# The last block's output projection by seven half-size products, and softmax sums moved to the head of their visit

## Chip, core and metric

The kernel runs on one core of a Trainium2 chip. The metric is the device time of one execution in microseconds (us). A core has five engines that run their own instruction streams in order and meet through semaphores: PE (matrix products), DVE (elementwise vector work), ACT (activations and copies), POOL (here broadcasts over partitions, and loads), and SP (here it only issues transfers). The profile shows PE's weight loads apart, as PEld.

## The reference

Linear attention in the style of Linformer, then a gated feed-forward layer. Batch 8, 8 heads, sequence 1024, head size 64; K and V are projected along the sequence to 64 rows.

```python
k_proj = np.einsum('ks,bhsd->bhkd', E, k)
v_proj = np.einsum('ks,bhsd->bhkd', F, v)
scores = scale * np.matmul(q, k_proj.transpose(0, 1, 3, 2))
attn = softmax(scores)            # over the 64 projected rows
x = np.matmul(attn, v_proj)       # heads side by side: 8192 tokens x 512
gate = 1.0 / (1.0 + np.exp(-(x @ w_gate)))
val = x @ w_val                   # 512 -> 1536, both
out = gate * val @ w_out          # 1536 -> 512, float32
```

## The kernel before

**Tiles and blocks.** The 8192 tokens are 16 blocks of 512, two blocks to a batch; `o1 = 2 * b` is the first block of batch `b`. For a block, the gate `x @ w_gate` is twelve groups of four 128x512 matmuls (`g_step`), and the value and output products are done by Strassen's scheme in Winograd's form: a 2x2 block product from seven half-size products instead of eight. For the value product these are `v_product` pieces (`p1`, `p26`, `p57`, `p4`, `p3`, lines 1461 to 1499). For the output product they are `product` calls of 12 matmuls with 256 columns each, in `first_products` and `last_products` (lines 1295 to 1328).

**Operands of the output product.** The hidden activations `hT` of a block are split into quarters: `A11`, `A21` hold the first 768 hidden features for tokens 0 to 255 and 256 to 511, `A12`, `A22` the other 768. `s_sums` (line 1214) makes four sums on DVE: S1 = A21 + A22, S2 = S1 - A11, a third that replaces A21 by A11 - A21 in place, and a fourth that replaces A12 by A12 - S2 in place. The sums can be made for part of the rows: `A = (0, 4)` for four of six row tiles, `Z = (4, 6)` for the last two. The matching sums T1 to T4 of `w_out` are made once. Partial results are taken out of PSUM as snapshots (`keep_snap`, ACT) and added to the output tile `ost` on DVE (`add_snap`, line 1277). Before the change the last block alone, number 15, uses plain products instead: `oproj` (line 1163) with 12 matmuls of 512 columns for each of four groups of 128 tokens, the fourth split into 384 and 128 columns.

**Order of the work.** Nothing is scheduled by a planner: the program is written out in order, each helper appends its instruction to its engine's stream, and `Plan` (line 28) works out the semaphore waits from keys that are read and written. The main loop (line 1610) runs `b` from 1 to 7. One iteration has six units of nine slots: `g_step` and the `v_product` pieces alternate, and `on(u, j, fn)` hangs further work behind slot `j` of unit `u`. In iteration `b`, this work is the output products of blocks `2b - 1` and `2b`, and the attention of batch `b + 1`, for `b` up to 6.

**The visit.** `outputs3` (line 1055) is hung on `on(3, 0, ...)`. On PE it issues the attention outputs `xo_one` for two head pairs, the softmax sums `den8`, and, in iterations 1 to 5, the K and V projection `kv` of the batch after. ACT copies the attention outputs to `xu` (`x_half`). DVE takes the reciprocals of the sums (`rec`, line 838). Then eight small transfers on SP bring the reciprocals to rows (`gather`), POOL broadcasts them over partitions (`spread`, line 912), and DVE multiplies `xu` by them into `xT` (`mul`, line 945), from slot (4, 4) on. `xT` is what the next batch's feed-forward reads. Ahead of `outputs3` in the same slot stand the `Z` sums of block `2b` (line 1657), three DVE instructions.

**Banks.** `FF` and `AA` are lists of free PSUM banks, four each. `take` pops the first; a bank is put back when its reader has been issued.

Of the kernel before, what the change touches and what calls it, by code (L numbers as in the profile page):

```python
# [7 lines left out]
ALU = mybir.AluOpType  # L8
# [9 lines left out]
DM = 512  # L18
# [100 lines left out]
def bass_linformer_attn__then__ffn_glu_sigmoid_kernel(  # L119
# [11 lines left out]
    B = q.shape[0]  # L131
# [6 lines left out]
    with contextlib.ExitStack() as es:  # L138
# [71 lines left out]
        ost = sbuf("ost", [P, 4, DM], FP32)  # L210
# [13 lines left out]
        add = plan.add  # L224
# [29 lines left out]
        FF, AA = Free(), Free()  # L254
# [15 lines left out]
        def dve(fn, r, w, b=None):  # L270
            x = [] if b is None else [("bank", b)]
            return add("DVE", fn, r=r, w=w, x=x)
# [525 lines left out]
        def attention(b):  # L798
# [127 lines left out]
            def xo_one(r, bks):  # L926
                for g in range(2):
                    n = 2 * r + g
                    for c in range(2):
                        kk = slice(64 * (g ^ c), 64 * (g ^ c) + 64)  # L930
                        mm(
                            bks[g],
                            bank[bks[g]][64 * c : 64 * c + 64, :],
                            vpD[kk, 2 * r + c, :],
                            eT[kk, n, :],
                            VPD(r // 2) + [("eT", n)],
                            tp=(64 * (g ^ c), 64 * c),
                        )
# [115 lines left out]

            def outputs3():
                f, a0 = FF.two(), AA.two()
                xo_one(2, f)
                xo_one(3, a0)
                bd = AA.take()
                den8(bd)  # L1060
                if b + 1 < B:
                    held["kv"] = AA.take()
                    kv(b + 1, held["kv"])
                for g in range(2):
                    x_half(2, g, f)
                    FF.append(f[g])
                later("A0", x_half, 3, a0, AA)
                rec(0)
                rec(1)
                AA.append(bd)  # L1070
                gather()
                spread(0)
                spread(1)
# [161 lines left out]
                return [(x, m) for m in up]  # L1235
            return [("hT", blk % 2, m + H6 * (x[2] == "2"), int(x[1]) - 1) for m in up]

        def product(blk, bk, A, B, start=False, stop=False):
            h = hT[blk % 2]
            for j in range(2):  # L1240
                for m in range(H6):
                    if A[0] == "S":
                        lhsT = hS[:, int(A[1]) - 1, m, j * P : (j + 1) * P]
                    else:
                        c = 256 * (A[1] == "2") + j * P
                        lhsT = h[:, m + H6 * (A[2] == "2"), c : c + P]
                    if B[0] == "T":
                        rhs, k = wT[:, int(B[1]) - 1, m, :], ("wT", int(B[1]) - 1)
                    else:
                        c = 256 * (B[2] == "2")  # L1250
                        rhs, k = wO[:, m + H6 * (B[1] == "2"), c : c + 256], "wO"
                    mm(
                        bk,
                        bank[bk][:, 256 * j : 256 * j + 256],
                        lhsT,
                        rhs,
                        part(blk, A, [m]) + [k],
                        start=start and m == 0 and j == 0,
                        stop=stop and m == H6 - 1 and j == 1,
                        read=True,  # L1260
                    )

# [50 lines left out]
        def last_products(blk):  # L1313
            a, c = chain
            product(blk, a, "A22", "T4", stop=True)
            o, keys = quarter(1, 0)
            act(o, bank[a][:, :].rearrange("p (j c) -> p j c", j=2), [], keys, b=a, scale=0.5)
            product(blk, c, "A12", "B22", stop=True)
            add_snap(1, c, 0, 1)
            AA.extend(chain)  # L1320
            for tt in (2, 3, 0, 1):
                t = 2 * (2 * (blk % 2) + tt % 2) + tt // 2
                add(
                    "SP",
                    lambda e, tt=tt, t=t: e.dma_start(out_v[blk // 2, t], ost[:, tt, :]),
                    r=[("ost", tt, n) for n in range(2)],
                    dma=f"out{tt}",
                )

# [278 lines left out]
        for b in range(1, B):  # L1610
            todo, at = [], {}
            for u in range(6):
                K = 6 * b + u
                p1, p26, p57, p4, p3 = v_pieces(K)
                todo += [
                    last_piece,
                    p1,
                    lambda K=K: g_step(K, 1),
                    p26,
                    lambda K=K: g_step(K, 2),  # L1620
                    p57,
                    lambda K=K: g_step(K, 3),
                    p4,
                    (lambda K=K: g_step(K + 1, 0)) if K + 1 < 6 * B else (lambda: None),
                ]
                last_piece = p3

            def on(u, j, fn):
                put(9 * u + j, fn)

            def h_sums(blk, ms, *ns):
                return lambda: [s_sums(blk, n, ms) for n in ns]

            def x_sums(blk, *ns):
                return lambda: [xs_sums(blk, n) for n in ns]

            A, Z = (0, 4), (4, 6)
            o0, o1 = 2 * b - 1, 2 * b
            if b == 1:
                first = {1: lambda: (vt_sums(1), vt_sums(4), x_sums(2, 1, 2, 3, 4)())}  # L1640
                on(0, 0, lambda: first_products(o0, first))
                on(0, 2, lambda: last_products(o0))
                on(0, 4, x_sums(3, 1, 2, 3, 4))
                on(2, 0, h_sums(o1, A, 1))
                on(2, 4, h_sums(o1, A, 2, 3))
            else:
                on(0, 4, h_sums(o0, A, 1, 2))
                on(1, 0, h_sums(o0, A, 3))
                on(1, 0, h_sums(o0, Z, 1))
                on(1, 4, h_sums(o0, Z, 2, 3))  # L1650
                first = {
                    0: x_sums(o1 + 1, 1, 2, 3, 4),
                    1: h_sums(o1, A, 1, 2, 3),
                }
                on(2, 0, lambda: first_products(o0, first))
                on(2, 2, lambda: last_products(o0))
            on(3, 0, h_sums(o1, Z, 1, 2, 3))
            if b + 1 < B:
                n = attention(b + 1)
                late, keep_kv, mul = n["late"], n["keep_kv"], n["mul"]  # L1660
                ks = 1 if b == 1 else 0
                for u, name in ((ks, "scores"), (ks + 1, "mixed")):
                    on(u, 0, n[name])
                    on(u, 1, lambda: late("A0", 0))
                    on(u, 3, lambda: late("A0", 1))
                    on(u, 6, lambda: (late("A1", 0), late("A1", 1)))
                on(3, 0, n["outputs"])
                on(3, 1, lambda: late("A0", 0))
                on(3, 3, lambda: late("A0", 1))
                on(3, 6, lambda: keep_kv(0))  # L1670
                on(4, 1, lambda: keep_kv(1))
                on(4, 3, lambda: keep_kv(2))

                on(4, 4, lambda: (mul(0, 0), mul(0, 1)))
                last = {
                    -1: lambda: mul(1, 0),
                    0: lambda: (mul(1, 1), mul(2, 0), mul(2, 1)),
                    1: lambda: (mul(3, 0), mul(3, 1)),
                }
                on(5, 0, lambda: first_products(o1, last))  # L1680
                on(5, 4, x_sums(o1 + 2, 1, 2))
                on(5, 7, x_sums(o1 + 2, 3, 4))
            else:
                on(5, 0, lambda: first_products(o1))
            on(5, 2, lambda: last_products(o1))
            if b + 2 < B:
                kpd_ = [("kpD", R) for R in range(2)] if b == 1 else []
                load_at = (1, 4) if b == 1 else (0, 2)
                on(*load_at, lambda: (load_k(b + 2, kpd_), load_v(b + 2), load_q(b + 2)))
                on(3, 4, transpose_q)  # L1690
            for i, slot in enumerate(todo):
                slot()
                for fn in at.pop(i, ()):
                    fn()
            assert not at
        last_piece()
        last = 2 * B - 1
        for tt in range(4):
            oproj(
                last,  # L1700
                tt,
                FF.take(),
                ((0, DM),) if tt < 3 else ((0, 384), (384, DM)),
            )

        plan.emit(nc, es, final=[f"out{i}" for i in range(4)] + ["outlast"])

# [26 lines left out]
```

## Time and profile before

| quantity | value |
| --- | --- |
| median of 7 runs | 535.78 us (534.55 to 536.32) |
| the profiled execution: its time | 535.89 us |
| the profiled execution: its span, first to last instruction | 534.1 us |
| PE busy | 521.4 us, 98% |
| DVE, ACT, POOL busy | 404.5, 300.6, 133.3 us |
| granted TensorE clock | 1.000 |

The rest of the profiled time beside the span lies before the first and after the last instruction. In a timeline line the columns are start (us from the span's start), duration (us), engine, source line, operation, output and inputs by name, shapes, how many instructions are merged, and in brackets the engine's idle time before them with what ended it. `SPq` is an issue of a transfer by SP, not the transfer. Almost all matmuls have line 264 and are told apart by their tiles: `pF<-xT,wG` is the gate, `pF<-xS,wV` and the like the value product, `pA<-wT,hS` and the like the output product, `pA<-eT,dsel` the softmax sums, `pF<-eT,vpD` the attention outputs, `pA<-KVs,EFT` the projection of K and V. A matmul's duration includes its way through the array, so starts, not ends, show PE's pace.

### The profile page before, as it was taken

The numbers are of one execution on the slowest core, as the hardware profiler recorded it, in microseconds if no ns is written. First come the engines' busy times: TensorE is split into PE (matmuls) and PEld (weight loads), VectorE is DVE, ScalarE is ACT, GpSimd is POOL, SyncE is SP. The second block draws the span as 40 slices with busy tenths as digits, with TensorE's granted clock in tenths as the row PEclk, the third lists the DMA queues.
The fourth block names the chain that finished last, engine by engine and source line by source line (L and its number), as shares of the span: only waits on it lengthen the run. The fifth ranks groups of instructions, "written<-read, shape, count | busy, mean of one in ns | idle before, by whom it ended". The sixth has DMA issues, their size and how long they took to land.

```text
span 534.1 us, 10316 instructions
## 1 busy us (share of the span) xinstructions
PE 521.4 (98%) x4113; PEld 344.4 (64%) x4113; DVE 404.5 (76%) x655; ACT 300.6 (56%) x540; POOL 133.3 (25%) x148
## 2 busy tenths in 40 slices
PE   5999999999999999999999999999999999999998
PEld 4544446656857667585766768576675856767674
DVE  3646386888987788877988789878888789887733
ACT  2554732687385564946567473755748464544540
POOL 9310200104800076001930048100650009200000
PEclk9999999999999999999999999999999999999999
DMA  9999999893295254921679223962520010202022
GB/s 167 199 192 202 162 201 217 148 180 64 37 225 84 79 92 71 227 57 45 91 154 162 80 45 56 202 108 80 91 80 1 14 69 3 79 1 80 1 79 80
DMA packets 76768, 56.18 MB, mean 105 GB/s; under 512 B 34800, under 2 KB 68528, under 8 KB 76720
## 3 DMA queue, kind: packets, MB, share of 16 engines
q0 software_dynamic: 33984, 29.89, 36.0%
q1 hardware_dynamic: 42736, 25.63, 19.7%
q8 instruction: 32, 0.52, 0.4%
q14 instruction: 16, 0.13, 0.1%
HBM read 60.29 MB, written 16.78 MB: 144 GB/s over the span
## 4 chain that ended last, share of the span: by engine, by line
PE 89%; DVE 5%; DMA 3%; POOL 1%; issue 1%; ACT 0%; DVEq 0%; POOLq 0%
PE pF L264 59%; PE pA L264 30%; DMA KVs<-in_v_dram 2%; DVE xT L949 2%; DVE vsnap L1435 2%; POOL KVs L917 1%; DVE rden L841 1%; DVE hT L1150 0%; POOL KVs L282 0%; DMA eT<-rden 0%; POOL Qb L282 0%; DVE hT L1416 0%; ACT vsnap L268 0%; DVE hS L1228 0%; DVE rden L639 0%
## 5 line engine op out<-in xcount | busy, mean ns | idle before, releaser
L264 PE MATMUL pF<-xT,wG 128*128 128x512 bf16 x768 | 197.9, 379 | 0.3
L917 POOL PARTITION_BROADCAST KVs<-eT x96 | 96.5, 1032 | 246.2 <-PE pF L264 193.4
L268 ACT ACTIVATE sig<-pF 128x512 f32<-128x512 f32 x192 | 115.6, 602 | 52.9 <-PE pF L264 50.9
L1435 DVE TENSOR_TENSOR vsnap<-pF,vsnap 128x512 f32<-128x512 f32 x126 | 86.7, 688 | 38.0 <-PE pF L264 27.5
L264 PEld LDWEIGHTS pF<-xT,wG 128*128 128x128 bf16 x768 | 73.7, 98 | 57.1 <-issue 1.7
L268 ACT ACTIVATE vsnap<-pF 128x512 f32<-128x512 f32 x126 | 75.3, 598 | 49.7 <-PE pF L264 46.9
L1416 DVE SCALAR_TENSOR_TENSOR hT<-sig,vsnap 128x512 bf16<-128x512 f32 x126 | 88.3, 701 | 6.2 <-ACT vsnap L268 0.5
L264 PE MATMUL pF<-xT,wV 128*128 128x256 bf16 (+1 forms) x432 | 76.1, 297 | 0.3 <-DVE hT L1150 0.3
L264 PE MATMUL pA<-wO,hT 128*128 128x256 bf16 x504 | 59.6, 273 | 0.0
L264 PEld LDWEIGHTS pF<-xT,wV 128*128 128x128 bf16 x432 | 40.6, 98 | 28.2 <-issue 4.9
L264 PEld LDWEIGHTS pA<-wO,hT 128*128 128x128 bf16 x504 | 49.3, 98 | 5.9
L264 PE MATMUL pF<-xS,wV 128*128 128x256 bf16 x336 | 50.5, 273 | 2.6 <-DVE vsnap L1435 2.0
L949 DVE TENSOR_TENSOR xT<-xu,KVs 128x512 bf16<-128x512 f32 x48 | 47.5, 1028 | 6.6 <-POOL KVs L917 6.6
L264 PE MATMUL pF<-xS,vT 128*128 128x256 bf16 x336 | 50.4, 273 | 0.0
L264 PEld LDWEIGHTS pF<-xS,wV 128*128 128x128 bf16 x336 | 31.9, 98 | 26.9 <-DVE vsnap L1435 9.0
L268 ACT ACTIVATE EF<-pA 128x512 f32<-128x512 f32 x28 | 16.7, 598 | 45.3 <-PE pA L264 45.3
L264 PE MATMUL pA<-wT,hT 128*128 128x256 bf16 x336 | 41.3, 273 | 0.0
L264 PE MATMUL pA<-wT,hS 128*128 128x256 bf16 x336 | 39.0, 273 | 0.0
L264 PEld LDWEIGHTS pA<-wT,hT 128*128 128x128 bf16 x336 | 32.9, 98 | 6.8
L264 PEld LDWEIGHTS pF<-xS,vT 128*128 128x128 bf16 x336 | 32.9, 98 | 3.8
L264 PEld LDWEIGHTS pA<-wT,hS 128*128 128x128 bf16 x336 | 32.5, 98 | 4.2
L1150 DVE SCALAR_TENSOR_TENSOR hT<-sig,pF 128x512 bf16<-128x512 f32 x24 | 16.4, 688 | 23.3 <-PE pF L264 11.2
(109 smaller groups left out, 501.8 us busy)
## 6 DMA issues: line engine op xcount, KB each, us to landing
out_dram<-ost SPq DMA_DIRECT2D x60, 256.0 KB, 2.5
Qb<-in_q_dram POOLq DMA_DIRECT2D x7, 1024.0 KB, 20.5
KVs<-in_k_dram POOLq DMA_DIRECT2D x7, 1024.0 KB, 12.7
KVs<-in_v_dram POOLq DMA_DIRECT2D x7, 1024.0 KB, 16.4
wO<-in_moe_w_out_dram POOLq DMA_DIRECT2D x1, 1536.0 KB, 13.0
wG<-in_moe_w_gate_dram POOLq DMA_DIRECT2D x5, 256.0 KB, 18.0
wV<-in_moe_w_val_dram POOLq DMA_DIRECT2D x5, 256.0 KB, 18.6
KVs<-in_k_dram POOLq DMA_DIRECT2D x2, 512.0 KB, 8.9
```

The lines of the kernel that those rows point to most:

```text
L264: return add("PE", lambda e: e.matmul(o, lhsT, rhs, **kw), r=r, x=[("bank", b)])
L268: return add("ACT", lambda e: e.activation(o, i, func, scale=scale), r=r, w=w, x=x)
L841: lambda e: e.reciprocal(rden[:, cc], bank[bk][:, cc]),
L917: lambda e, n=n, i=2 * rnd + c, j=j, parts=parts: e.partition_broadcast(rb[0:parts, n, :], rrow[32 * j : 32 * j + 1, i, :], channels=parts),
L949: lambda e: e.tensor_tensor(xT[s][:, r, :, 256 * g : 256 * g + 256], xu[:, n, :].rearrange("p (f c) -> p f c", f=2), y.rearrange("p (f c) ...
L1150: lambda e: e.scalar_tensor_tensor(hT[blk % 2][:, m, :], sg, 1.0, bank[pv][:, :], ALU.add, ALU.mult,),
L1416: lambda e: e.scalar_tensor_tensor(o, sg[:, :, cc], 1.0, x.rearrange("p (j c) -> p j c", j=2), ALU.add, ALU.mult,),
L1435: lambda e: e.tensor_tensor(o, bank[bk][:, :], o, ALU.add),
```

## The change

Three things are changed. In `outputs3`, `den8` is issued ahead of both `xo_one`. The `Z` sums of block `2b` are appended after `outputs3`, so that on DVE they follow the reciprocals; in iteration 6 they are hung four slots later; in iteration 7, which has no attention, they stay. And block 15 is done by seven products too: its operand sums are made inside iteration 7, and `final_products` takes the place of `oproj`. Its order differs from the other blocks': it uses five banks, one product of A12 and B22 is issued in two halves (`js`), each into a bank of its own, and the output leaves in eight stores of 128 rows by 256 columns instead of five.

```diff
--- before.py
+++ after.py
@@ -1054,10 +1054,10 @@
 
             def outputs3():
                 f, a0 = FF.two(), AA.two()
+                bd = AA.take()
+                den8(bd)
                 xo_one(2, f)
                 xo_one(3, a0)
-                bd = AA.take()
-                den8(bd)
                 if b + 1 < B:
                     held["kv"] = AA.take()
                     kv(b + 1, held["kv"])
@@ -1235,9 +1235,9 @@
                 return [(x, m) for m in up]
             return [("hT", blk % 2, m + H6 * (x[2] == "2"), int(x[1]) - 1) for m in up]
 
-        def product(blk, bk, A, B, start=False, stop=False):
+        def product(blk, bk, A, B, start=False, stop=False, js=(0, 1)):
             h = hT[blk % 2]
-            for j in range(2):
+            for j in js:
                 for m in range(H6):
                     if A[0] == "S":
                         lhsT = hS[:, int(A[1]) - 1, m, j * P : (j + 1) * P]
@@ -1255,8 +1255,8 @@
                         lhsT,
                         rhs,
                         part(blk, A, [m]) + [k],
-                        start=start and m == 0 and j == 0,
-                        stop=stop and m == H6 - 1 and j == 1,
+                        start=start and m == 0 and j == js[0],
+                        stop=stop and m == H6 - 1 and j == js[-1],
                         read=True,
                     )
 
@@ -1326,6 +1326,54 @@
                     r=[("ost", tt, n) for n in range(2)],
                     dma=f"out{tt}",
                 )
+
+        def final_products(blk):
+
+            a, b, c, e0 = [AA.take() for _ in range(4)]
+            e1 = FF.take()
+
+            def store(tt, col, sem):
+                t = 2 * (2 * (blk % 2) + tt % 2) + tt // 2
+                cc = slice(256 * col, 256 * col + 256)
+                add(
+                    "SP",
+                    lambda e: e.dma_start(out_v[blk // 2, t][:, cc], ost[:, tt, cc]),
+                    r=[("ost", tt, col)],
+                    dma=sem,
+                )
+
+            def plus(o, keys, n, bk, jj):
+                dve(
+                    lambda e: e.scalar_tensor_tensor(
+                        o, bank[bk][:, jj], 0.5, snap[n][:, jj], ALU.mult, ALU.add
+                    ),
+                    [("snap", n)],
+                    keys,
+                    b=bk,
+                )
+
+            product(blk, a, "A11", "B11", True)
+            keep_snap(0, a)
+            product(blk, c, "S1", "T1", True, True)
+            product(blk, a, "S2", "T2")
+            keep_snap(1, a)
+            plus(snap[1], [("snap", 1)], 1, c, slice(0, 512))
+            product(blk, b, "A12", "B21", True, True)
+            s_sums(blk, 4, (0, 6))
+            add_snap(0, b, 0, 0)
+            product(blk, a, "A21", "T3")
+            keep_snap(2, a)
+            add_snap(2, c, 1, 1)
+            product(blk, e0, "A12", "B22", True, True, (0,))
+            plus(ost[:, 0, 256:512], [("ost", 0, 1)], 1, e0, slice(0, 256))
+            product(blk, a, "A22", "T4", stop=True)
+            o, keys = quarter(1, 0)
+            act(o, bank[a][:, :].rearrange("p (j c) -> p j c", j=2), [], keys, b=a, scale=0.5)
+            product(blk, e1, "A12", "B22", True, True, (1,))
+            plus(ost[:, 1, 256:512], [("ost", 1, 1)], 1, e1, slice(256, 512))
+            for tt, col in ((0, 0), (1, 0), (2, 1), (3, 1), (0, 1), (2, 0), (3, 0)):
+                store(tt, col, f"out{tt}")
+            store(1, 1, "outlast")
 
 
 
@@ -1654,7 +1702,6 @@
                 }
                 on(2, 0, lambda: first_products(o0, first))
                 on(2, 2, lambda: last_products(o0))
-            on(3, 0, h_sums(o1, Z, 1, 2, 3))
             if b + 1 < B:
                 n = attention(b + 1)
                 late, keep_kv, mul = n["late"], n["keep_kv"], n["mul"]
@@ -1665,6 +1712,7 @@
                     on(u, 3, lambda: late("A0", 1))
                     on(u, 6, lambda: (late("A1", 0), late("A1", 1)))
                 on(3, 0, n["outputs"])
+                on(3, 0 if b + 2 < B else 4, h_sums(o1, Z, 1, 2, 3))
                 on(3, 1, lambda: late("A0", 0))
                 on(3, 3, lambda: late("A0", 1))
                 on(3, 6, lambda: keep_kv(0))
@@ -1681,7 +1729,10 @@
                 on(5, 4, x_sums(o1 + 2, 1, 2))
                 on(5, 7, x_sums(o1 + 2, 3, 4))
             else:
-                on(5, 0, lambda: first_products(o1))
+                on(3, 0, h_sums(o1, Z, 1, 2, 3))
+                last = {1: h_sums(o1 + 1, A, 1, 2, 3)}
+                on(5, 0, lambda: first_products(o1, last))
+                on(5, 7, h_sums(o1 + 1, Z, 1, 2, 3))
             on(5, 2, lambda: last_products(o1))
             if b + 2 < B:
                 kpd_ = [("kpD", R) for R in range(2)] if b == 1 else []
@@ -1694,14 +1745,7 @@
                     fn()
             assert not at
         last_piece()
-        last = 2 * B - 1
-        for tt in range(4):
-            oproj(
-                last,
-                tt,
-                FF.take(),
-                ((0, DM),) if tt < 3 else ((0, 384), (384, DM)),
-            )
+        final_products(2 * B - 1)
 
         plan.emit(nc, es, final=[f"out{i}" for i in range(4)] + ["outlast"])
 
```

## The prediction

> **What bounds the kernel now.** I read the page first (busy shares, chain), then the timeline around one attention visit of the main loop (iteration 4) and around the last one (iteration 6), then the end of the program. From the page:
>
> ```profile
> span 534.1 us, 10316 instructions
> ...
> PE 521.4 (98%) x4113; PEld 344.4 (64%) x4113; DVE 404.5 (76%) x655; ACT 300.6 (56%) x540; POOL 133.3 (25%) x148
> ...
> PE 89%; DVE 5%; DMA 3%; POOL 1%; issue 1%; ACT 0%; DVEq 0%; POOLq 0%
> ```
>
> PE is the bound, so an edit pays only where PE issues fewer columns or stands still. Standstill is read from start times: twelve 256-column matmuls occupy 1.31 us (one product starts at 421.13, its follower at 422.44), four 512-column ones 0.87 (422.88 to 423.75); anything beyond that before the next start is a stall. The usual visit (timeline, iteration 4):
>
> ```profile
> 308.77 1.76 DVE L841 RECIPROCAL rden<-pA 128x128 f32<-128x128 f32 x2
> ...
> 310.56 5.56 SPq L904 DMA_DIRECT2D eT<-rden  x8
> ...
> 311.17 0.69 DVE L1435 TENSOR_TENSOR vsnap<-pF,vsnap 128x512 f32<-128x512 f32 x1 [0.64 <-PE pF L264]
> ...
> 319.17 2.21 DVE L949 TENSOR_TENSOR xT<-xu,KVs 128x512 bf16<-128x512 f32 x2
> ```
>
> Here the `vsnap` add after the reciprocals waits 0.64 for PE, so their place costs nothing, and the first `xT` multiply has no wait for POOL. PE loses only 0.23 us after the multiplies (512-column group at 320.94, +0.87 = 321.81, next start 322.04). The last visit (iteration 6) has no K/V projection behind it, 1.9 us of PE work elsewhere:
>
> ```profile
> 434.24 1.76 DVE L841 RECIPROCAL rden<-pA 128x128 f32<-128x128 f32 x2
> ...
> 434.96 1.03 PE L264 MATMUL pF<-xT,wG 128*128 128x512 bf16 x4
> ...
> 435.92 0.63 DVE L1435 TENSOR_TENSOR vsnap<-pF,vsnap 128x512 f32<-128x512 f32 x1
> 436.03 5.58 SPq L904 DMA_DIRECT2D eT<-rden  x8
> ...
> 436.61 0.61 PE L264 MATMUL pF<-xS,wV 128*128 128x256 bf16 x4 [0.62 <-DVE vsnap L1435]
> ...
> 439.99 0.95 POOL L917 PARTITION_BROADCAST KVs<-eT  x1 [45.29 <-issue]
> ...
> 444.36 2.10 DVE L949 TENSOR_TENSOR xT<-xu,KVs 128x512 bf16<-128x512 f32 x2 [0.70 <-POOL KVs L917]
> ...
> 446.38 0.68 DVE L1435 TENSOR_TENSOR vsnap<-pF,vsnap 128x512 f32<-128x512 f32 x1
> ...
> 447.11 0.61 PE L264 MATMUL pF<-xS,wV 128*128 128x256 bf16 x4 [0.79 <-DVE vsnap L1435]
> ```
>
> PE stalls twice: 434.96 + 0.87 = 435.83 against 436.61, 0.78 us; and (group at 445.30) 446.17 against 447.11, 0.94 us. Both hang on the reciprocals: the first because the add queues behind them, the second through gather, broadcast, multiply (which did wait 0.70 for POOL) and the add behind the multiplies. The end (timeline, then SP's last issue):
>
> ```profile
> 520.90 10.55 PE L264 MATMUL pF<-wO,hT 128*128 128x512 bf16 x60
> ...
> 524.49 7.80 SPq L1191 DMA_DIRECT2D out_dram<-ost  x5
> ...
> 530.90 0.89 DVE L1181 TENSOR_SCALAR ost<-pF 128x384 f32<-128x384 f32 x2 [1.26 <-PE pF L264]
> ```
> ```profile
> 531.86 0.43 SPq L1191 DMA_DIRECT2D out_dram<-ost  x1
> ```
>
> So what counts at the end is when SP can start its last store, 531.86; the span ends 2.2 us later.
>
> **What the Trainium skill says.** "TensorE: Matmul & The Clock Gate", Back-to-back issue gap, gives N/2.4 + 2.5 ns: 109 and 216 ns for 256 and 512 columns; the trace has 1.31/12 = 109 and 0.87/4 = 217. "Perfetto Trace Analysis", DMA Instruction — HWDGE (DVE, Sync): SP is held from semaphores met until descriptors are made, then is free. The trace agrees: stores start 300.49 and 300.87, taking 0.33 and 0.43, so about 0.38 then 0.48 us a store back to back. "DMA: Bandwidth & Descriptors", Anatomy of one DMA: most of the fixed time is the write receipt; the trace's 64 KB store lands in 1.7 us, the 256 KB ones in 2.5, so small stores keep their tail. "SBUF — State Buffer", Who interferes with whom: a DVE instruction with two SBUF inputs collides with a GpSimd one that reads SBUF; the `xT` multiplies take 1.14 us (median) in the broadcasts, 0.68 at least without.
>
> **The change, part by part.**
> *den8 ahead of xo, six visits.* Same matmuls, same number of changes of tile shape (about 0.1 us each: the 16 den8 matmuls start at 306.76, kv at 307.31). The xo products, and the ACT copies of `xu`, come 0.55 us later; ACT's next work in iteration 4 is at 309.86, and in iteration 6 its queue catches up by 435.2. Cost 0; unhidden, 0.55 in a visit.
>
> *Reciprocals ahead of the operand sums (five visits), sums to a later slot (sixth).* The three sums cost DVE 1.13 us (433.11 to 434.24); the reciprocals start that much earlier: den8's result is there by about 432.3, DVE's previous instruction lets go at 433.11. In iterations 1 to 5 the add's 0.64 us wait for PE covers the exchange, and the multiplies are placed by DVE, not POOL. Gain 0; I bound it at -0.1 to +0.1 a visit (the broadcasts now begin 1.1 us earlier, over other two-input instructions).
> In iteration 6 the add goes from 435.92 to 434.79, ends 435.47, before PE's 435.83: the 0.78 goes. All eight gather issues, and so the broadcasts, come 1.13 earlier. PE is 0.78 earlier, so the second stall shrinks by 1.13 - 0.78 = 0.35, to about 0.59. The sums land behind the next `hT` multiply, from 436.0 to 437.1, where DVE then waits for ACT anyway (0.97 us before, 437.34 to 438.32); the following add can start at 437.54 either way. If that cover failed, PE would meet it when bank c is needed again, 0.65 us further on. Gain 1.13; bounds 0.6 (half the sums come through) and 1.72 (both stalls gone).
>
> *Sums of block 15.* Four-row sums, 3 x 0.69 = 2.05 us, go where DVE waits 2.60 us (513.87 to 516.47): 0. The two-row sums, 1.13 us, precede DVE's last two `vsnap`/`hT` steps; `A12` is then whole at about 524.1 and is read at 525.3: 0.
>
> *Last block.* Removed: 36 x 512, 12 x 384, 12 x 128 columns; added: 84 x 256. PE issue: 520.90 to 531.29 (10.39) becomes 84 x 0.109 = 9.17. Step by step from 520.90, 1.31 each: A11 to 522.21, S1 523.52, S2 524.83, A12·B21 526.14, A21 527.45. The sum that rewrites `A12` waits for PE (0.30 from product end to DVE start, as at 508.42 and 508.72), 526.44 + 0.95 = 527.39: just in time for the half product, 528.10. A22·T4 needs the third snapshot: 527.45 + 0.20 + 0.60 = 528.25, a stall of 0.2. It ends 529.61, the second half product 530.27. DVE's last add, 256 wide (between 0.29 for 128 and 0.56 for 384, I take 0.43), 530.47 to 530.90.
> SP now has eight stores instead of five: ready at 528.03 (two), 528.97 (two), 529.3 (one), 530.45 (two, from ACT: 529.61 + 0.2 + 0.6), 530.90. With 0.38 and 0.48 spacing: 530.48, 530.86, and the last at 531.34 instead of 531.86: 0.5 earlier; its 128 KB queue behind less data than the 192 KB before, I add 0.1. Gain 0.6 of PE's 1.22; bounds 0.75 (SP never waits) and -0.2 (0.6 us an issue, as the gather's: 529.0 + 5 x 0.6 = 532.0).
>
> Sum: 1.13 + 0.6 = 1.73 on the profiled 535.89, 534.16; the median of the runs is 0.11 lower, so **534.05 us**.
>
> **Rivals.** (a) *The stores take the last block's gain.* At 0.57 us an issue the last starts at 529.0 + 2.85 = 531.85, as before. For: the eight gather issues take 5.58, some spaced 0.59. Against: those carry waits for one another, stores show 0.38 to 0.5. Time 535.78 - 1.13 = 534.65.
> (b) *The moved sums or late `xu` copies come through in iteration 6*, 0.5 us of the 1.13 lost. Against: the 0.97 of DVE idle. Time 534.55.
> (c) *Slower: the store queue outright.* From 0.80 us an issue (5 x 0.80 + 529.0 = 533.0) the end loses more than the 1.13 gained; at 1.1 us, 534.5 for the last store, 2.6 later: 535.78 - 1.13 + 2.6 = 537.3. For it: only SP's transposes take over 1.2 us; plain stores never.
> (d) *The usual visits gain too*, the 0.23 stall gone in each of five: 534.05 - 1.15 = 532.9. Against: nothing there waits for POOL.
> (e) *The last block's dependent tail costs more* (each product waits for its snapshot), gain 0: near 534.65 too, with (a).
>
> **How the numbers follow.** Forecast 0.60; (a) with (e) 0.17; (b) 0.11; (c) 0.06; (d) 0.06. A measurement can tell about 0.2%, 1.07 us: faster means under 534.71. The forecast lies under it but for about a twelfth (0.05 of 0.60, by the lower bounds), (d) wholly, (a) and (b) by little, so about half of them: 0.55 + 0.06 + 0.14 = 0.75. Same: 0.05 + 0.14 = 0.19; slower 0.06. Range: down to 535.78 - 1.72 - 0.75 = 533.3; up to -0.2 at the end with 0.8 in iteration 6, 535.2.
>
> **What would show it.** Right: the add in iteration 6 at about 434.8, no PE stall there, the later one near 0.6; visits 1 to 5 stall 0.23 as before; PE's last matmul starts about 1.0 earlier on its own stage and SP's last store about 0.5. Wrong: stores spaced 0.57 or more; PE waiting over 0.4 in the last seven products; a new stall behind the sums in iteration 6.

## The result and the profile after

| | before | after |
| --- | --- | --- |
| median | 535.84 us (60 runs) | 534.37 us (25 runs) |
| ratio, 95% interval | | 0.9974 (0.9967 to 0.998) |
| profiled execution: span | 534.1 us | 532.1 us |

The changed kernel is faster by 1.47 us, 0.26%; 534.05 was forecast. The two profiled executions differ by more, 2.0 us, because their first loads took different times: the first gate matmul starts at 21.41 us in one and at 20.88 in the other. All comparisons of profiles below therefore count from a matmul of their own, and a stretch is compared with the same stretch.

From the page of the changed kernel:

```profile
span 532.1 us, 10382 instructions
...
PE 520.4 (98%) x4137; PEld 347.9 (65%) x4137; DVE 407.4 (77%) x662; ACT 302.9 (57%) x544; POOL 133.5 (25%) x148
...
PE 93%; DVE 3%; DMA 1%; issue 1%; POOL 1%; ACT 0%; SPq 0%; POOLq 0%; DVEq 0%
```

PE is the bound still; DVE's share of the chain fell from 5% to 3%. The usual visit, iteration 4, in the timeline after:

```profile
306.89 1.76 DVE L841 RECIPROCAL rden<-pA 128x128 f32<-128x128 f32 x2
...
308.68 5.55 SPq L904 DMA_DIRECT2D eT<-rden  x8
...
310.42 0.69 DVE L1483 TENSOR_TENSOR vsnap<-pF,vsnap 128x512 f32<-128x512 f32 x1 [0.69 <-PE pF L264]
...
318.34 2.22 DVE L949 TENSOR_TENSOR xT<-xu,KVs 128x512 bf16<-128x512 f32 x2
```

The `vsnap` add still waits for PE (0.69) and the multiply for nothing. Iteration 6:

```profile
432.22 1.76 DVE L841 RECIPROCAL rden<-pA 128x128 f32<-128x128 f32 x2
...
433.90 0.69 DVE L1483 TENSOR_TENSOR vsnap<-pF,vsnap 128x512 f32<-128x512 f32 x1
434.01 5.58 SPq L904 DMA_DIRECT2D eT<-rden  x8
434.07 1.03 PE L264 MATMUL pF<-xT,wG 128*128 128x512 bf16 x4
...
434.93 0.60 PE L264 MATMUL pF<-xS,wV 128*128 128x256 bf16 x4
...
437.91 0.69 DVE L1464 SCALAR_TENSOR_TENSOR hT<-sig,vsnap 128x512 bf16<-128x512 f32 x1
...
437.98 1.28 POOL L917 PARTITION_BROADCAST KVs<-eT  x1 [45.22 <-issue]
...
442.67 2.10 DVE L949 TENSOR_TENSOR xT<-xu,KVs 128x512 bf16<-128x512 f32 x2 [0.70 <-POOL KVs L917]
...
445.43 0.61 PE L264 MATMUL pF<-xS,wV 128*128 128x256 bf16 x4 [0.79 <-DVE vsnap L1483]
```

The gate group at 434.07 is followed at 434.93, 0.86 later: the first stall, 0.78 us, is gone. The second is as long as before: the multiply waits 0.70 for POOL, as it did, and PE 0.79, a stall of 0.95 us by start times. The end:

```profile
525.77 0.82 PE L264 MATMUL pA<-wO,hT 128*128 128x256 bf16 x6
525.97 0.60 ACT L268 ACTIVATE snap<-pA 128x512 f32<-128x512 f32 x1 [1.96 <-PE pA L264]
526.32 3.85 SPq L1340 DMA_DIRECT2D out_dram<-ost  x8
...
526.62 1.48 PE L264 MATMUL pA<-wT,hT 128*128 128x256 bf16 x12
...
528.80 0.42 DVE L1347 SCALAR_TENSOR_TENSOR ost<-pF,EF 128x256 f32<-128x256 f32 x1 [1.18 <-PE pF L264]
```

The eight issues run from 526.32 to 530.17. The whole difference can be laid out in three stretches, each between starts of matmuls that both kernels have:

| stretch | before | after | gain |
| --- | --- | --- | --- |
| first gate matmul to the visit of iteration 6 | 410.26 | 409.89 | 0.37 |
| that visit to the last value product (4 matmuls, `pF<-xS,wV`) | 88.79 | 88.00 | 0.79 |
| last value product to the end of the span | 13.63 | 13.32 | 0.31 |

The sum is 1.47 us. The medians differ by as much, but the interval of their ratio allows 1.07 to 1.77 us, so the agreement to the hundredth is chance. The first row is five usual visits at about 0.075: an iteration takes 62.66 instead of 62.73, because the stall behind the multiplies is 0.16 there instead of 0.24.

### The profile page after: what moved, and what is told of

The parts are those of the page before. It is cut to its first block, busy times and chain, and to the rows that moved or that the text cites. A ratio compares the mean times of both kernels' runs of the same rounds, so it can differ in the third digit from the quotient of the medians.

```text
span 532.1 us, 10382 instructions
## 1 busy us (share of the span) xinstructions
PE 520.4 (98%) x4137; PEld 347.9 (65%) x4137; DVE 407.4 (77%) x662; ACT 302.9 (57%) x544; POOL 133.5 (25%) x148
## 4 chain that ended last, share of the span: by engine, by line
PE 93%; DVE 3%; DMA 1%; issue 1%; POOL 1%; ACT 0%; SPq 0%; POOLq 0%; DVEq 0%
PE pF L264 60%; PE pA L264 32%; DMA EF<-in_F_dram 1%; POOL KVs L917 1%; DVE xT L949 1%; DVE rden L841 1%; DVE vsnap L1483 1%; DVE hT L1150 0%; DMA eT<-rden 0%; DVE rden L639 0%; DVE hS L1228 0%; DVE xT L688 0%; DVE ost L1280 0%; ACT qT L268 0%; ACT vsnap L268 0%
## 5 line engine op out<-in xcount | busy, mean ns | idle before, releaser
L1464 DVE SCALAR_TENSOR_TENSOR hT<-sig,vsnap 128x512 bf16<-128x512 f32 x126 | 87.1, 691 | 6.2 <-ACT vsnap L268 0.5
L264 PE MATMUL pA<-wO,hT 128*128 128x256 bf16 x534 | 63.4, 273 | 0.0
L264 PEld LDWEIGHTS pA<-wO,hT 128*128 128x128 bf16 x534 | 52.2, 98 | 6.3
L268 ACT ACTIVATE EF<-pA 128x512 f32<-128x512 f32 x30 | 17.9, 598 | 48.9 <-PE pA L264 48.9
L264 PE MATMUL pA<-wT,hT 128*128 128x256 bf16 x360 | 44.2, 273 | 0.0
L264 PE MATMUL pA<-wT,hS 128*128 128x256 bf16 x360 | 41.8, 273 | 0.0
L264 PEld LDWEIGHTS pA<-wT,hT 128*128 128x128 bf16 x360 | 35.2, 98 | 7.3 <-ACT snap L268 0.3
L264 PEld LDWEIGHTS pA<-wT,hS 128*128 128x128 bf16 x360 | 35.2, 98 | 4.1
L1280 DVE SCALAR_TENSOR_TENSOR ost<-pA,EF 128x512 f32<-128x512 f32 x29 | 20.0, 688 | 20.4 <-PE pA L264 20.4
```

Source lines behind the costliest of these rows:

```text
L264: return add("PE", lambda e: e.matmul(o, lhsT, rhs, **kw), r=r, x=[("bank", b)])
L268: return add("ACT", lambda e: e.activation(o, i, func, scale=scale), r=r, w=w, x=x)
L1280: lambda e: e.scalar_tensor_tensor(o, bank[bk][:, :].rearrange("p (j c) -> p j c", j=2), 0.5, snap[n].rearrange("p (j c) -> p j c", j=2), ...
L1464: lambda e: e.scalar_tensor_tensor(o, sg[:, :, cc], 1.0, x.rearrange("p (j c) -> p j c", j=2), ALU.add, ALU.mult,),
```

## The experiments

The theory after the comparison: these three gains are separate and add; in iteration 6 the 0.35 that should have come from the second stall was lost in the first broadcast, which started while a DVE instruction with two SBUF inputs was running and waited for it; at the end PE's gain is lost to the stores. Rivals: the prediction's own sum (1.13 and 0.6); one part doing all; a broadcast set by the gather's transfers; a tail that only counts issues, or only bytes. All kernels below keep the computation whole.

**The visits alone, and the last block alone.** The first takes the old `oproj` loop back:

```diff
-        final_products(2 * B - 1)
+        last = 2 * B - 1
+        for tt in range(4):
+            oproj(
+                last,
+                tt,
+                FF.take(),
+                ((0, DM),) if tt < 3 else ((0, 384), (384, DM)),
+            )
```

with iteration 7's sums for block 15 left out.

> The changed kernel with the old last block: block 15 by plain products of 512 columns, without its operand sums; only the visits are changed. Theory of the parts: the two parts add. The visits give 0.78 us in iteration 6 (first PE stall gone, second unchanged at 0.95) and 0.08 us in each of iterations 1 to 5, 1.16 in all, so a ratio to the kernel before of about 0.9978. Rival, the sum of the prediction: 1.13 us, all in iteration 6, with the second stall near 0.6. Rival, one part does all: 0 or the full 1.47 us. In the profile: DVE's multiplies in the usual visits preceded by an hT step of 0.69 us rather than 0.77, PE stall there 0.16 rather than 0.24.

The second keeps the last block and puts the visit back:

```diff
+                on(3, 0, h_sums(o1, Z, 1, 2, 3))
                 on(3, 0, n["outputs"])
-                on(3, 0 if b + 2 < B else 4, h_sums(o1, Z, 1, 2, 3))
```

and `den8` behind both `xo_one`.

> Only the last block is changed; visits as in the kernel before. Theory of the parts: from the last value product's start to the end of the span 13.31 us instead of 13.63, so 0.32 us faster, ratio 0.9994, at the edge of what is seen. Prediction's working: 0.6 us. Rival: PE's 1.2 us fewer of issue all arrive, 1.2 us. In the profile: SP's last store about 0.46 us earlier after that product's start, and the time from that store to the end 0.14 longer.

Measured: 0.9967 (0.9956 to 0.9978) for the visits alone, 0.9994 (0.9985 to 1.0004) for the last block alone, which is no difference by its times. The stretches are sharper: to the visit of iteration 6, 409.86 and 410.22 us; from there to the last value product, 87.98 and 88.80; to the end, 13.64 and 13.31. Each half of the change has its own rows of the table and none of the other's. The parts add, and the last block by itself is worth 0.3 us, not PE's 1.2. From here on the evidence is the stretches, of one profiled execution each: the changed kernel and the four that differ from it only in `den8` or in the last block take 87.98 to 88.00 us in the second one, and all that keep the last block and its eight stores on SP take 13.31 to 13.32 us in the third. By the times alone, none of the single edits below can be told from the changed kernel; the intervals overlap.

**The softmax sums back behind the attention outputs**, the rest as changed:

```diff
                 f, a0 = FF.two(), AA.two()
-                bd = AA.take()
-                den8(bd)
                 xo_one(2, f)
                 xo_one(3, a0)
+                bd = AA.take()
+                den8(bd)
```

> The changed kernel with the softmax sums back behind the attention outputs on PE; operand sums still after the reciprocals. Theory: in iteration 6 the softmax sums are done about 0.55 us later, near the time at which DVE is free for the reciprocals, so the first stall stays gone and the time is that of the changed kernel within 0.1 us. Rival: the lead of the softmax sums is what frees DVE, and 0.5 us or more of the gain is lost. The reciprocals in iteration 6 start no more than 0.1 us later against the visit's start.

Measured: 0.9968 (0.9957 to 0.998), 533.93 us; from the visit of iteration 6 to the last value product 87.98, to the changed kernel's 88.00. So the lead of `den8` on PE contributes nothing here: the reciprocals of iteration 6 start 1.48 us after the visit's start, 1.44 in the changed kernel, so 0.55 us of delay on PE is hidden but for 0.04 behind the DVE instruction before them. What works is the order on DVE.

**Iteration 6's sums directly behind its reciprocals.**

```diff
-                on(3, 0 if b + 2 < B else 4, h_sums(o1, Z, 1, 2, 3))
+                on(3, 0, h_sums(o1, Z, 1, 2, 3))
```

> The changed kernel with iteration 6's operand sums in the visit's own slot, directly behind the reciprocals, rather than four slots later. Theory: the vsnap add again queues behind 1.13 us of sums, so the first stall of 0.78 us returns; but then PE is later and the broadcasts are 1.1 us early against it, so the multiplies no longer wait for POOL and the second stall falls from 0.95 to about 0.2. Time within 0.15 us of the changed kernel. Rival: the second stall stays at 0.95 because DVE's own chain sets it, and the kernel is 0.78 us slower than the changed one.

Measured: 0.9971 (0.9961 to 0.9981), 534.4 us. From the timeline of this kernel:

```profile
434.46 0.36 DVE L1228 TENSOR_TENSOR hS<-hT 128x512 bf16<-128x512 bf16 x1
...
435.53 0.68 DVE L1483 TENSOR_TENSOR vsnap<-pF,vsnap 128x512 f32<-128x512 f32 x1
...
436.27 0.61 PE L264 MATMUL pF<-xS,wV 128*128 128x256 bf16 x4 [0.61 <-DVE vsnap L1483]
...
438.54 0.80 POOL L917 PARTITION_BROADCAST KVs<-eT  x1 [45.22 <-issue]
...
443.25 2.21 DVE L949 TENSOR_TENSOR xT<-xu,KVs 128x512 bf16<-128x512 f32 x2
```

The first stall is back (0.78 by start times), the first broadcast is short, the multiply waits for nothing, and the second stall is 0.29. The stretch takes 88.11, 0.11 more than in the changed kernel. The multiply starts 11.91 us after the visit's start, 11.90 in the changed kernel: it is no earlier, PE comes to it later. So the two stalls are not separate gains. PE restarts behind the second one when the multiplies and the add behind them are done, 15.44 us after the visit's start in the kernel before, 14.66 in the changed one and 14.78 here. What iteration 6 gains is this lead of the multiplies, and it comes from the earlier reciprocals; the later slot for the sums adds only the 0.11.

**Two DVE instructions of iteration 6 exchanged**, in `p4`, unit 39 alone:

```diff
+                if K == 39:
+                    hidden(K, 1, 1, vsnap[2][:, :], [("vsnap", 2)])
                 hidden(K, 0, 1, bank[a][:, :], [], b=a)
                 FF.append(a)
-                hidden(K, 1, 1, vsnap[2][:, :], [("vsnap", 2)])
+                if K != 39:
+                    hidden(K, 1, 1, vsnap[2][:, :], [("vsnap", 2)])
```

> The changed kernel with two DVE instructions of iteration 6 exchanged: the hT step with two SBUF inputs (sig, vsnap) goes ahead of the one that reads PSUM, so that it is over when the first broadcast starts. Theory of the shared port: the first broadcast, 1.28 us in the changed kernel, takes 0.7 to 0.8 as in the usual visits, the first multiply starts about 0.5 earlier and the second stall falls from 0.95 to about 0.5; about 0.45 us faster than the changed kernel, and than the kernel before by 1.9. Rival: the broadcast's length comes from the transfers of the gather or from POOL's own start, stays at 0.95 to 1.28, and nothing is gained.

Measured: 0.9969 (0.9957 to 0.9981), 533.94 us; too near the changed kernel's 0.9974 for the times to part them, but the timeline is plain:

```profile
438.01 0.69 DVE L1464 SCALAR_TENSOR_TENSOR hT<-sig,vsnap 128x512 bf16<-128x512 f32 x1 [0.17 <-ACT sig L268]
...
438.49 0.88 POOL L917 PARTITION_BROADCAST KVs<-eT  x1 [45.22 <-issue]
438.62 0.68 DVE L1464 SCALAR_TENSOR_TENSOR hT<-sig,pF 128x512 bf16<-128x512 f32 x1
...
442.63 2.21 DVE L949 TENSOR_TENSOR xT<-xu,KVs 128x512 bf16<-128x512 f32 x2
...
445.50 0.61 PE L264 MATMUL pF<-xS,wV 128*128 128x256 bf16 x4 [0.34 <-DVE vsnap L1483]
```

The first broadcast takes 0.88 instead of 1.28, the multiply has no wait for POOL any more, PE's stall is 0.50 instead of 0.95, and the stretch is 87.54 instead of 88.00. The gather was not touched. The second broadcast is shorter too, 0.80 instead of 1.24, because no DVE instruction with two SBUF inputs is running when it starts; so the exchange removes a delay that the kernel before had as well (1.24), and not only the one that the change brought. The first broadcast's end follows the two-input DVE instruction's end: in the kernel before, 440.28 and 440.94; changed, 438.59 and 439.26; here 438.70 and 439.36. That is 0.66 us each time, whether the broadcast then shows as 0.95, 1.28 or 0.88. The same holds for every broadcast of this kind (line 917) in the twelve traces, 96 in each: 864 of 1152 begin while such a DVE instruction runs or in the same 2 ns, and end 0.66 to 0.67 us after it; the other 288 take 0.79 to 0.80. This agrees with the Trainium skill, "SBUF — State Buffer", Who interferes with whom: a DVE instruction with two SBUF inputs contends with a GpSimd instruction that reads SBUF, over a pair of ports that is an exclusive lock.

**Fewer stores, and stores from two queues.** One kernel joins the stores of two token groups that become ready together:

```diff
-            for tt, col in ((0, 0), (1, 0), (2, 1), (3, 1), (0, 1), (2, 0), (3, 0)):
-                store(tt, col, f"out{tt}")
+            store2(0, 0, "out0")
+            store2(1, 1, "out2")
+            store(0, 1, "out1")
+            store2(1, 0, "out3")
             store(1, 1, "outlast")
```

where `store2` (its definition is left out here) moves `ost[:, 2 * tok : 2 * tok + 2]` of one column half in one transfer.

> The changed kernel with the eight last stores merged into five: one transfer for each pair of token groups that becomes ready together. Theory of the issue queue: the last store waits for one issue less, starting about 0.38 to 0.47 earlier against the last products, and the end gains about 0.4. Rival, the data: 1 KB rows set the end whatever the number of issues, the larger transfer takes as long to issue and drain, and the gain is under 0.1.

The other lets ACT issue the two stores of the quarter that it evicts (`store` gets the engine as a fourth argument, left out here):

```diff
-                store(tt, col, f"out{tt}")
+                store(tt, col, f"out{tt}", "ACT" if tt > 1 and col == 0 else "SP")
```

> The changed kernel with the two stores of the quarter that ACT evicts issued by ACT itself, the other six by SP. Theory of the issue queue: SP's last store starts when DVE's last add is done, about 0.45 earlier against the last products, and the end gains 0.3 to 0.45. Rival, the data: the transfers share the same engines, the last one's data starts no earlier than the others have drained, and the gain is under 0.1.

Measured: 0.9967 (0.9954 to 0.9979), 533.51 us, and 0.9973 (0.9966 to 0.9981), 534.04 us. The stretch from the last value product to the end takes 13.13 and 13.21 us, after 13.32 in the changed kernel. From the two timelines, SP and ACT at the end (the first two lines are of the five stores):

```profile
528.55 0.37 SPq L1380 DMA_DIRECT2D out_dram<-ost  x1
...
528.97 0.47 SPq L1340 DMA_DIRECT2D out_dram<-ost  x1
```
```profile
528.89 1.39 SPq L1340 DMA_DIRECT2D out_dram<-ost  x2
529.55 0.86 ACTq L1340 DMA_DIRECT2D out_dram<-ost  x2
```

| | before | changed | five stores | two queues |
| --- | --- | --- | --- | --- |
| last value product to SP's last issue | 11.40 | 10.95 | 10.49 | 10.48 |
| SP's last issue to the end of the span | 2.23 | 2.38 | 2.64 | 2.73 |
| sum | 13.63 | 13.32 | 13.13 | 13.21 |

The issue comes 0.46 earlier in both, as the issue theory has it, but 0.26 and 0.35 of that return behind it. The gain is 0.19 with five stores, half-way between the two theories, and 0.11 with two queues, near the rival's. The packets of the traces show why: with the queue relieved, the last 384 KB leave the DMA engines back to back (529.43 to 530.72 us with five stores, 530.41 to 531.71 with two queues, 0.43 us for 128 KB), and the last store's data starts about 1.26 us after its issue, behind the two before it; in the changed kernel it is 0.97. Less data behind the last product may shorten this further; that was not tried.

**Iteration 7's sums later too.**

```diff
             else:
-                on(3, 0, h_sums(o1, Z, 1, 2, 3))
+                on(3, 4, h_sums(o1, Z, 1, 2, 3))
```

> The changed kernel with iteration 7's two-row operand sums moved four slots later too, as the change did in iteration 6. Theory: the vsnap add no longer queues behind the sums, so iteration 7's stall of 0.37 us goes, and the sums fit DVE's idle 0.97 us before its next add; 0.37 us faster than the changed kernel, 1.85 than before. Rival: the sums reappear as a stall further on, no gain.

Measured: 0.9967 (0.9954 to 0.998), 533.75 us. The stretch from iteration 6's visit is 87.60, 0.40 shorter. In the changed kernel the add follows the last of the sums and PE waits for it; then the same place in this kernel:

```profile
493.04 0.42 DVE L1228 TENSOR_TENSOR hT<-hT 128x512 bf16<-128x512 bf16 x1
...
493.38 0.68 DVE L1483 TENSOR_TENSOR vsnap<-pF,vsnap 128x512 f32<-128x512 f32 x1
...
494.12 0.61 PE L264 MATMUL pF<-xS,wV 128*128 128x256 bf16 x4 [0.21 <-DVE vsnap L1483]
```

```profile
492.27 0.69 DVE L1483 TENSOR_TENSOR vsnap<-pF,vsnap 128x512 f32<-128x512 f32 x1 [0.39 <-PE pF L264]
...
493.68 0.42 DVE L1228 TENSOR_TENSOR hS<-hT 128x512 bf16<-128x512 bf16 x1
...
495.00 0.69 DVE L1483 TENSOR_TENSOR vsnap<-pF,vsnap 128x512 f32<-128x512 f32 x1
```

The add at 492.27 now waits for PE instead of keeping it waiting (0.37 us of stall by start times in the changed kernel), and the sums fill what was idle time of DVE.

**The three edits together, and the changed kernel once more beside it.**

> The changed kernel with the exchange of the two hT steps in iteration 6, iteration 7's sums four slots later, and five last stores. Theory: they touch different stalls and add, 0.45 + 0.37 + 0.2 = 1.0 us faster than the changed kernel, 2.5 us faster than the kernel before, ratio 0.9953. Rival: the stall that is taken away in iteration 6 or 7 reappears behind, and less than half of the 1.0 us arrives. In the profile: stalls 0.5 and 0 in iterations 6 and 7, first broadcast below 0.9 us, 13.13 us from the last value product to the end.

> The changed kernel itself, unedited, beside the one before it here, so that both are timed on one chip: 1.0 us slower than the three edits together if those add, and 1.47 us faster than the kernel before.

Measured: 532.94 us, 0.9952 (0.9939 to 0.9966), against 534.09, 0.997 (0.9959 to 0.9982). The stretches: 87.17 against 88.00, and 13.14 against 13.32, so 1.0 us in all, as expected; the medians differ by 1.15. The two stalls aimed at are 0.50 and none. Two others in iteration 7, which the study left alone, are as long as in the kernel before: 0.44 us where the vsnap add stands behind another of the operand sums, and 0.28 before the last value product. This is the fastest kernel of the study, 2.5 us below the one before.

## Why the prediction was right, and where it was off

The direction, the size and the two places were right; the size was right in part because two terms that were too large met one that was too small: 1.73 was forecast, 0.35 and 0.29 of it did not come, and 0.37 came where nothing was expected.

*den8 ahead of xo: 0.* Right, and shown: with `den8` put back, the same stretches.

*Sums of block 15: 0.* Right: the second stretch is 87.98 us without them (the visits alone) and 88.00 with them.

*Usual visits: 0, bounds -0.1 to +0.1 each.* Inside the bounds, but in the same direction five times, 0.37 us. The `hT` step ahead of the multiplies takes 0.69 instead of 0.77 (changed: 317.73 to 318.42), so the multiplies and the add behind them begin that much sooner. The runs tie it to the order on DVE: the stall is about 0.16 with the visits alone and with `den8` put back, about 0.24 with the last block alone. The traces show why. First the kernel before, then the changed one, iteration 4:

```profile
318.05 0.80 POOL L917 PARTITION_BROADCAST KVs<-eT  x1
...
318.48 0.77 DVE L1416 SCALAR_TENSOR_TENSOR hT<-sig,vsnap 128x512 bf16<-128x512 f32 x1
```
```profile
317.07 0.80 POOL L917 PARTITION_BROADCAST KVs<-eT  x1
...
317.73 0.69 DVE L1464 SCALAR_TENSOR_TENSOR hT<-sig,vsnap 128x512 bf16<-128x512 f32 x1
```

The step starts while a broadcast runs, 0.37 us before that broadcast's end in the kernel before and 0.14 in the changed one, in all five visits. Over the twelve traces the `hT` steps with two SBUF inputs and the multiplies that start 0.3 us or more before a broadcast's end finish 0.40 to 0.41 us after that end, all 475; the 161 that start 0.21 or less before it take no longer than 0.70. So the broadcasts, which come earlier against DVE, no longer hold this step up. The prediction had named the shifted broadcasts as the reason for its bounds, but had not drawn the sum over five.

*Iteration 6, first stall: 0.78.* It went, and its cover held: the sums end at 436.52, and the next add starts at 436.63, when ACT's snapshot is there. But that the gain equals this stall to the hundredth is chance: with the stall put back the kernel loses only 0.11. The gain is the lead of the multiplies, 0.79.

*Iteration 6, second stall: 0.35.* Nothing came. The step "all eight gather issues, and so the broadcasts, come 1.13 earlier" held for the gather and for the start of the first broadcast (1.12 earlier against the visit), but this broadcast took 1.28 instead of 0.95. It met the two-input `hT` step for 0.6 us rather than 0.3. So its end, and with it the multiplies, came only 0.79 earlier, and PE came 0.78 earlier: nothing was left for this stall. The rule that two-input instructions and broadcasts collide was used in the prediction for the multiplies and the usual visits, but not for the first broadcast of iteration 6. The exchange of two instructions brought 0.46.

*Last block: 0.6.* The chain on the engines was right: against the first final matmul the A12·B21 product starts at 3.93 us, the stall ahead of A22·T4 is 0.20, and DVE's last add ends at 10.00 us, as worked out. SP's last issue is at 10.50, worked out at 10.44. Wrong was the term behind it: "its 128 KB queue behind less data than the 192 KB before, I add 0.1". The last store moves twice the bytes of the one before the change, 128 KB instead of 64. Its data starts 0.97 us after its issue, its last packet ends 1.49 us after it instead of 1.35, and from there to the landing it is about 0.39 in both. From issue to end of span it is 2.38 where it was 2.23: 0.15 lost instead of 0.1 won. So 0.31 came.

*The rivals.* "The stores take the last block's gain" was half of what happened, but not by slower issues: they were spaced 0.38 and 0.5 where nothing else held them, read before as 0.38 and 0.48. The sums did not come through in iteration 6. No store of the last block took longer than 0.46 us to issue. The usual visits did gain, but 0.07 of their 0.23 each. The last block's chain of products cost no more than was worked out.

## What to carry to other kernels

When an early result is meant to start another engine sooner, look at what that engine's first instruction will run beside at its new time: here 0.33 us of a 1.12 us lead went into one port collision, and exchanging two instructions took 0.46 out of this collision and the next. A stall that disappears is not yet a gain: if PE waits again soon after, only an earlier end of that wait counts. A chain of stores at the end has two prices, the issues and the drain (the time in which their data leaves); removing issues moved more than half of the time to the drain here. That the pieces behind the last product should be small in bytes as well as few follows from this, but was not tried. Where a queue holds work that is due much later (the operand sums), moving it behind the next instruction that is due soon cost nothing here, where the queue has an idle gap before the one after; it was worth 0.4 us in iteration 7, which the change had left out.

## What the hardware showed beyond the expected

A broadcast over partitions that starts during a DVE instruction with two SBUF inputs ends 0.66 us after that instruction, to the hundredth or so in all twelve traces, and 0.79 us after its own start without one; it is held back, not slowed in proportion. The other way round, such an instruction that starts well inside a broadcast ends 0.40 us after it. Three queued stores of 128 KB in 1 KB rows leave in 0.43 us each, whether one or two queues issued them; the eight that SP alone issues in the changed kernel leave in about 0.5 each.
